# Loads of two chunks moved ahead of a weight load, and other places for a key transpose and for POOL's multiplications, in an RWKV attention with a cosine feed-forward

## The chip, the cores and the metric

The kernel runs on one core of one Trainium2 chip. The metric is the device time of one execution in microseconds, the median of several runs. A core has five engines that work side by side, each through its own queue in order: TensorE (PE, the matmuls), VectorE (DVE), ScalarE (ACT), GpSimd (POOL) and SyncE (SP), which issues the loads and stores here. Loads from one queue are spread over 16 DMA engines, called the rings below.

## The reference

Two parts follow each other. The first is a linear attention with decay over 4 batches, 8 heads, 768 steps and 48 numbers per head; the second takes its output, 3072 tokens of 384 numbers, through two matrices with g = h * cos(h) between them.

```python
for t in range(S):
    kt, vt, rt, wt = (k[:, :, t], v[:, :, t], r[:, :, t], w[:, :, t])
    cur = np.einsum('bhd,bhe->bhde', u[None] * kt, vt)
    y[:, :, t] = np.einsum('bhd,bhde->bhe', rt, state + cur)
    state = wt[:, :, :, None] * state + np.einsum('bhd,bhe->bhde', kt, vt)
...
h = x @ w_in            # 3072 x 384 times 384 x 2048
return (h * np.cos(h)) @ w_out
```

All is float32.

## The kernel before

The steps are cut into 24 chunks of 128 (6 per batch, taken batch by batch within each chunk number, so chunks 0 to 3 are the first of their batches and have no state before them). Two chunks make a block of 256 tokens, and there are 12 blocks.

Attention per chunk j: a load `tt` (L248) holds r, k and w transposed; `v` (L266) holds v; `rk` (L262) holds r and k in natural order for the bonus term with u; `u_sb` (L260) is u, loaded once with the first rk. VectorE makes running products of w from both ends with two scans (e and f in the tables), multiplies r and k by them (r, k), TensorE makes the scores (a, L374 or L382), and VectorE puts them over the diagonal (P). The diagonal comes from r * k (m, L320), times u (u, L321), summed per head on VectorE (c, L325), and spread over a matrix by two selects on POOL (A, L335). For chunks from 4 on, m and u are the only two instructions for the bonus, on POOL in the early part and on VectorE later. The keys are also needed with time on the rows: for chunks from 4 on this is done with 16 small DMAs per chunk (t, L425) and one transpose of 32 x 32 blocks on VectorE (K, L429, output `kn`). The state of a block is made by 64 matmuls from kn and v (s, L444, output `pst`), 32 for each of the two chunks; the block's attention output by o (L479, L485) and p (L507, L513).

Feed-forward per block: 8 units of 256 hidden numbers. A unit is 18 matmuls `ph` (mm1, L594), a chain of five steps I, S, N, M (ScalarE, VectorE, ScalarE, VectorE: rounding to a period, reduction, sine, product), H and L (the result `gs` as a high part, from ScalarE or VectorE, and a low part of two instructions, from POOL, L174), and 12 matmuls `acc` (mm2, L612), of which the first 8 take the high and the last 4 the low part. M frees the PSUM bank that the unit after the next writes. Each float32 operand is split into a high and a low part, therefore three passes per product.

Weights: 16 pieces `raw` of 768 KB (L180), brought into place by two instructions on ScalarE (wg, L195, and wl, L191), a combination on VectorE (wy, L203), a high part (wc, L171) and a low part (wx, L205). Only five pieces of raw memory exist, so that a raw load waits until the piece before it at its place has been converted: weight 14 takes weight 9's place.

The order is written out by hand. For the first two blocks it is the string `START`, whose tokens issue the steps in turn on PE, DVE, ACT and POOL, and the loads on SP. `ld4` is chunk 4's tt load, `v4` its v load, `lr5` chunk 5's rk load with u in front of it if it is the first, `raw14` a weight load; `m5 u5 c5 A5` are the bonus steps of chunk 5. After that, one row per unit of `FIRST` (blocks of the second pass) and then `PLAN`, where `K+3` means K of the chunk 3 behind the block's first. Behind START a scheduler chooses the place of the loads on SP's queue, among them the loads of v and tt for chunks 8 and 9, which `lv+4 lv+5 load+4 load+5` in the first row of FIRST ask for. Buffers are handed out in turn (5 for tt, 4 for v), and a load waits for the last reader of what was there.

The step that prepares a mask for the later chunks hangs on one token:

```python
if n == "u" and j == ALL_OF - 1:
    nc.gpsimd.tensor_copy(out=turned_mask, in_=mask)
```

Of the kernel before, what the change touches and what calls it, by code (L numbers as in the profile page):

```python
# [46 lines left out]
ALL_OF = 6  # L47
# [19 lines left out]
ld0 e0 f0 ld1 raw2 raw1 q0 e1 k0 D14 pc0 r0 q1 cd0 v0 v1 raw0 f1 D10 a0 W0 wg2 wl2 A0 k1 pc1 wl1 r1 wy2 P0 cd1 D6 a1  # L67
wc2 t0 wg1 A1 ld3 ld2 wg0 W1 t1 P1 v5 wx2 wy1 o0 K0 K1 xh0.0 xp0.0 s0 wl0 e3 q3 wc1 xa0.0 wy0 wc0 xh0.1 wp1 f3 pc3
xp0.1 wv1 wx0 xa0.1 q2 e2 n0 k3 f2 raw3 k2 m0.0 m1.0 pc2 t3 r3 I0 r2 wg3 raw4 v2 wl3 cd2 v3 raw5 wy3 m0.1 cd3 S0 t2 a3
A3 K3 K2 A2 P3 ld7 wl4 wg4 a2 ld5 wc3 wg5 N0 raw8 raw6 P2 s1 wx3 raw9 n1 o1 xh1.0 xl1.0 raw7 m1.1 xh1.1 xl1.1 M0 m0.2  # L70
wl5 Wa3 I1 wy4 m1.2 S1 m0.3 H0 wc4 N1 wy5 wc5 wg6 I2 m1.3 M1 wx4 wl6 I3 Hv1 L0 mm2.0 m0.4 wx5 S2 N2 wy6 S3 wg9 wl9 M2
m1.4 N3 L1 mm2.1 H2 I4 e5 wc6 wy9 L2 m0.5 M3 m1.5 S4 H3 wx6 N4 wg7 raw14 v4 L3 ld4 lr5 M4 raw11 m0.6 mm2.2 wl7 wcv9
wy7 wx9 mm2.3 wg8 I5 S5 wc7 wx7 H4 N5 M5 k5 m1.6 m0.7 raw10 W2 wl8 wg11 I6 m1.7 H5 wy8 L4 mm2.4 S6 wc8 L5 I7 N6 S7 N7
wl11 wx8 M6 mm2.5 H6 M7 H7 m0.8 m1.8 m5 u5 wl10 L6 I8 wg10 c5 f5 wy11 m0.9 L7 S8 e4 ld6 raw13 raw12 lr4 m1.9 N8 M8 I9
wc11 wy10 wg12 wc10 mm2.6 mm2.7 raw15 t5 d4 S9 N9 H8 A5 r5 wx11 a5 wx10 M9 wl12 wl13 H9 L8 L9 m0.10 wy12 wc12 m1.10
wg13 m0.11 I10 k4 P5 wx12 S10 m1.11 N10 mm2.8 I11 wy13 M10 wg15 wl15 Wa5 wc13 W4 m4 u4 d5 S11 c4 f4 wx13 N11 M11 m0.12
r4 H10 A4 L10 wg14 mm2.9 m1.12 m0.13 Hv11 K5 t4 wl14 I12 S12 N12 pp4 pp5 m1.13 a4 P4 wy15 L11 I13 M12 wy14 wcv15 S13
wx15 mm2.10 wc14 o2 mm2.11 N13 wx14 p2 m0.14 H12 m1.14 M13 m0.15 L12 xh2.0 Hv13 e6 k6 t6 m1.15 I14 S14 K4 N14 M14
mm2.12 I15 S15 xl2.0 L13 Hv14 L14 mm2.13 xh2.1 N15 s2 xl2.1 M15 Hv15 L15 n2
# [9 lines left out]
LAST = "mm1 I S N M", "mm1 I S N M mm2 h l", "mm2 h l"  # L89
# [7 lines left out]
def rwkv_cos_ffn(ctx: ExitStack, tc: tile.TileContext, tr, tn, tv, u, ut, wts, w, rkw, vst, us, xs, out):  # L97
# [78 lines left out]
    def fetch_weights(f):  # L176

        place = NF + 1 - RING + (f - 1) % RING
        raw[f] = wt.tile([128, 4 * DM], I32, tag=f"w{place}", name="raw")
        E["qf"].dma_start(out=raw[f].bitcast(I16)[:, :8 * DM - 1], in_=wts[f, :, 1:])  # L180
# [55 lines left out]
    def chunk(j):  # L236

        if j not in atts:
            atts[j] = {"j": j, "g": order[j], "b": order[j] // NCB, "c": order[j] % NCB}
        return atts[j]  # L240

    def att_load(j):
        a = chunk(j)
        g = a["g"]
        a["tt"] = tt = buf("tt", [C, TRW], F32)
        half = 1024 + NP // 2 * 129
        for cols in (*(((half, TRW), (1024, half)) if not atts_loaded else ((1024, TRW),)), (512, 1024), (0, 512)) if j < IN_PARTS else ((0, TRW),):
            E["qt"].dma_start(out=tt[:, slice(*cols)], in_=tr[g, :, slice(*cols)])  # L248
        a["tt"] = tt = tt[:R]
        a["r3"] = tt[:, 0:512].rearrange("p (a t) -> p a t", a=NP)  # L250
        a["k3"] = tt[:, 512:1024].rearrange("p (a t) -> p a t", a=NP)
        a["halves"] = not atts_loaded
        atts_loaded.append(j)
        if j == 0:
            E["qt"].dma_start(out=u_by_head, in_=ut)
# [382 lines left out]
    for i in PAIR:  # L638
# [7 lines left out]
                 a=att_scores, t=att_transpose, s=att_state, o=att_own, p=att_past, x=att_x)  # L646
# [64 lines left out]
    def at_first(token):  # L711

        by = re.match(r"(W|H|wc)([av])(\d+)$", token)
        if by:
            name = dict(W="whole", H="gh", wc="whi0")[by[1]]
            usual, E[name] = E[name], dict(a=nc.scalar, v=nc.vector)[by[2]]
            parts.pop((by[1], int(by[3])))()
            E[name] = usual
            return
        if token[:2] == "wp":  # L720
            parts.pop(("wx", int(token[2:])))
        if token[:2] == "wx":
            for x in "wp", "wv":
                parts.pop((x, int(token[2:])))
        if token[:2] == "xp":
            parts.pop(("xl", (int(token[2]), int(token[4]))))
        if token[:2] == "xl":
            for x in "xp", "xa":
                parts.pop((x, (int(token[2]), int(token[4]))))
        n, at, side = re.match(r"(mm2\.|m[01]\.|[a-zA-Z]+)(\d+)(?:\.(\d))?$", token).groups()  # L730
        j = int(at)
        if n == "ld":
            att_load(j)
            att_decay(atts[j])
            seen.update({(j, "load"), (j, "decay"), (j, "x")})
        elif n == "D":
            tags = BANKS[stage[0]]["h"]
            filled = ps.tile([C, C], F32, tag=tags[(turn["h"] + 1) % len(tags)], name="filled")
            for again in range(j):
                nc.tensor.matmul(out=filled, lhsT=ident, rhs=ident, start=True, stop=True)  # L740
        elif n == "raw":
            fetch_weights(j)
            load_weights(j)
        elif n in ("v", "lr"):
            steps[{"v": "lv", "lr": "lr"}[n]](chunk(j))
            seen.add((j, {"v": "lv", "lr": "lr"}[n]))
            if n == "lr":
                att_diag(chunk(j))
                seen.add((j, "diag"))
        elif n == "pc":  # L750
            att_diag(atts[j])
            seen.add((j, "diag"))
        elif n in ("a", "t"):
            steps[n](atts[j])
            seen.add((j, n))
        elif n in ("o", "p", "s"):
            steps[n](j)
            seen.add((j, n))
            if n == "o" and atts[j * BLK]["c"] == 0:
                att_past(j)  # L760
                seen.add((j, "p"))
        elif n in ("m0.", "m1."):
            mm1(j, int(n[1]))
        elif n == "mm2.":
            mm2(j)
        else:
            if n == "d":
                att_dstate(atts[j])
                seen.add((j, "d"))
            parts.pop((n, (j, int(side)) if side else j))()  # L770
            if n == "u" and j == ALL_OF - 1:
                nc.gpsimd.tensor_copy(out=turned_mask, in_=mask)
                nc.gpsimd.memset(turned_mask[:ROW, TURNED:, ROW:], 0)
                nc.gpsimd.memset(turned_mask[ROW:, TURNED:, :ROW], 1)
# [23 lines left out]
    with tc.manual_schedule(engines={ET.PE, ET.DVE, ET.Activation, ET.Pool}):  # L798
# [6 lines left out]
        for t in range(up2, slots + LAG):  # L805
            n = t - up2
# [187 lines left out]
```

## Time and profile before

| what | value |
|---|---|
| median of 3 runs | 506.35 us (505.32 to 506.54) |
| profiled execution, its span | 506.66 us, 505.0 us |
| PE busy | 490.1 us, 97% of the span, 5560 instructions |
| DVE busy | 391.8 us, 78% |
| ACT busy | 257.9 us, 51% |
| POOL busy | 214.3 us, 42% |
| granted PE clock, mean | 0.997 |
| the chain that ended last | PE 82%, DVE 6%, POOL 5%, ACT 4% |

The times of an instruction come from the profiled execution alone. A busy share is a mean over the whole span: the first 100 us, in which weights are converted and two blocks run interleaved, look different from the ten blocks after them, which repeat every 39 us. In the page's row of granted clock all 40 slices show 9 (that is 90% or more of the full speed) but one, which shows 8: the slice from 139 to 151 us.

### The profile page before, as it was taken

Reading aid. Unit: us, or ns where it says so; the run is one execution under the profiler, and the core shown is the slowest. Engines: PE = TensorE matmul, PEld = TensorE weight load, DVE = VectorE, ACT = ScalarE, POOL = GpSimd, SP = SyncE. Lnnn points to the kernel's source line nnn. Section 1 sums busy time; section 2 is a strip of 40 time slices with the busy share of each in tenths; the row PEclk is TensorE's granted clock in tenths of the full one; section 3 lists DMA queues with packets and bytes.
Section 4 is the critical chain, followed back from the end, with each engine's and each line's share of the span. In section 5 each row is a group of like instructions: output and inputs, shape, how many; then the busy total and the mean of one; then the engine's idle time right before and its main releaser. Section 6 shows DMA issues by size and latency. Waiting matters only on the chain.

```text
span 505.0 us, 13533 instructions
## 1 busy us (share of the span) xinstructions
PE 490.1 (97%) x5560; PEld 474.6 (94%) x5560; DVE 391.8 (78%) x684; ACT 257.9 (51%) x443; POOL 214.3 (42%) x278
## 2 busy tenths in 40 slices
PE   8999898999899999999999999999999999999996
PEld 8889897899899999999999999999999999999996
DVE  8999699987959868967967967966967966587632
ACT  3899687435435445445345445435534444544542
POOL 5136399425435244433533524524523633432330
PEclk9999999999989999999999999999999999999999
DMA  8993933423443250351342332233214203023001
GB/s 281 414 394 140 374 100 95 125 57 107 131 143 106 48 193 18 78 160 53 78 143 70 79 102 110 78 85 127 75 42 155 64 4 124 31 65 126 33 1 35
DMA packets 46289, 58.59 MB, mean 116 GB/s; under 512 B 30736, under 2 KB 37392, under 8 KB 46224
## 3 DMA queue, kind: packets, MB, share of 16 engines
q1 hardware_dynamic: 46080, 57.59, 34.6%
q8 instruction: 45, 0.74, 0.6%
q14 instruction: 20, 0.16, 0.1%
q10 hardware_dynamic: 144, 0.10, 0.1%
HBM read 49.80 MB, written 4.72 MB: 108 GB/s over the span
## 4 chain that ended last, share of the span: by engine, by line
PE 82%; DVE 6%; POOL 5%; ACT 4%; issue 3%; DVEq 0%; ACTq 0%; POOLq 0%
PE ph L594 35%; PE acc L612 34%; POOL gs L174 3%; PE pa L382 2%; PE py L479 2%; PE filled L740 2%; PE py L485 2%; PE py L513 1%; PE pst L444 1%; DVE rr L560 1%; PE pa L374 1%; PE py L507 1%; POOL asb L335 1%; DVE tt L289 1%; ACT gs L171 1%
## 5 line engine op out<-in xcount | busy, mean ns | idle before, releaser
L174 POOL TENSOR_TENSOR gs<-rr,gs 128x256 fp32r<-128x256 f32 x188 | 159.0, 867 | 228.1 <-ACT gs L171 221.5
L594 PE MATMUL ph<-xT,w 128*128 128x256 f32 x1728 | 221.6, 282 | 4.2 <-DVE rr L574 2.9
L594 PEld LDWEIGHTS ph<-xT,w 128*128 128x128 f32 x1728 | 213.8, 189 | 8.5 <-issue 4.1
L612 PE MATMUL acc<-w,gs 128*128 128x384 f32 x1152 | 215.4, 337 | 0.7 <-ACT gs L171 0.7
L612 PEld LDWEIGHTS acc<-w,gs 128*128 128x128 f32 x1152 | 196.3, 188 | 1.3 <-ACT gs L171 1.0
L573 ACT ACTIVATE rr<-rr,quarter 128x512 f32<-128x512 f32 x96 | 69.5, 724 | 87.8 <-DVE rr L560 87.8
L560 DVE SCALAR_TENSOR_TENSOR rr<-rr,ph 128x512 f32<-128x512 int32 x96 | 65.5, 682 | 55.4 <-ACT rr L557 54.8
L171 ACT CAST gs<-rr 128x512 fp32r<-128x512 f32 x91 | 56.5, 621 | 71.1 <-DVE rr L574 51.2
L574 DVE TENSOR_TENSOR rr<-rr,ph 128x512 f32<-128x512 f32 x96 | 65.0, 678 | 21.2 <-ACT rr L573 19.3
L557 ACT ACTIVATE rr<-ph 128x512 int32<-128x512 f32 x96 | 57.2, 596 | 46.5 <-PE ph L594 46.1
L335 POOL TENSOR_SCALAR_AFFINE_SELECT asb<-cd 128x512 f32<-128x512 f32 x48 | 38.3, 823 | 47.7 <-DVE cd L325 28.5
L396 DVE COPY_PREDICATED asb<-turned_mask,pa 64x128 f32<-64x128 uint8 (+1 forms) x108 | 33.6, 346 | 2.1 <-POOL asb L335 0.3
L283 DVE TENSOR_TENSOR_SCAN ee<-tt,one_e 112x516 f32<-112x516 f32 (+1 forms) x25 | 32.4, 1298 | 1.2 <-DMA tt<-tr 1.0
L289 DVE TENSOR_TENSOR_SCAN tt<-tt,inj 112x516 f32<-112x516 f32 x24 | 30.3, 1262 | 0.8
L174 DVE TENSOR_TENSOR xT<-py,xT 128x384 fp32r<-128x384 f32 x22 | 11.5, 552 | 18.4 <-ACT xT L171 18.3
L195 ACT ACTIVATE top<-raw 128x768 f16<-128x768 bf16 x16 | 17.4, 1085 | 6.8 <-DMA raw<-wts 6.1
L479 PE MATMUL py<-asb,v 128*32 128x128 f32 x384 | 18.0, 276 | 0.3 <-DVE asb L393 0.2
L171 ACT CAST xT<-py 128x384 fp32r<-128x384 f32 x24 | 10.7, 481 | 14.5 <-PE py L513 10.2
L485 PE MATMUL py<-asb,v 128*32 128x128 f32 x384 | 17.3, 273 | 0.0
L203 DVE CUSTOM_DVE_ANT_0 h<-h,top 128x1536 uint16<-128x1536 uint16 x16 | 15.6, 973 | 0.7 <-ACT h L191 0.6
L171 ACT COPY past<-dd 48x192 f32<-48x192 f32 x40 | 14.0, 349 | 2.7 <-DVE dd L358 2.4
L382 PEld LDWEIGHTS pa<-tt 48*64 48x64 f32 x576 | 12.9, 133 | 2.2 <-issue 2.2
(93 smaller groups left out, 355.7 us busy)
## 6 DMA issues: line engine op xcount, KB each, us to landing
tt<-tr SPq DMA_DIRECT2D x22, 770.5 KB, 6.5
raw<-wts SPq DMA_DIRECT2D x16, 767.8 KB, 8.3
rk<-tn SPq DMA_DIRECT2D x20, 384.0 KB, 4.4
v<-tv SPq DMA_DIRECT2D x24, 224.0 KB, 3.8
ww<-w SPq DMA_DIRECT2D x6, 768.0 KB, 5.1
out<-ob SPq DMA_DIRECT2D x23, 192.0 KB, 2.0
top<-tt SPq DMA_DIRECT2D x112, 16.0 KB, 1.8
top<-tt SPq DMA_DIRECT2D x112, 8.0 KB, 1.8
```

What stands on the lines that cost most here:

```text
L171: (nc.scalar.copy if E[name] is nc.scalar else E[name].tensor_copy)(out=out, in_=in_)
L174: E[name].tensor_tensor(out=out, in0=full, in1=high.bitcast(F32), op=ALU.subtract)
L283: nc.vector.tensor_tensor_scan(out=ee[:, pairs].rearrange("p a t -> p (a t)")[:, ::-1], data0=wp[:, cols][:, ::-1], data1=one_e[:, pairs]. ...
L289: nc.vector.tensor_tensor_scan(out=wp[:, 0:W129], data0=wp[:, 0:W129], data1=inj.rearrange("p a t -> p (a t)"), initial=0.0, op0=ALU.mult, ...
L335: nc.gpsimd.affine_select(out=asb, in_=col.unsqueeze(2).to_broadcast([C, NP, C]), pattern=[[0, 4], [1, C]], compare_op=ALU.is_equal, fill= ...
L396: nc.vector.copy_predicated(*(which(x) for x in (a["asb", h], turned_mask, pa[h])))
L557: nc.scalar.activation(made["rr"].bitcast(I32), ph, AF.Copy, scale=INV2PI / W_SCALE, bias=0.25)
L560: nc.vector.scalar_tensor_tensor(out=made["rr"], in0=made["rr"].bitcast(I32), scalar=-2.0 * math.pi * W_SCALE, in1=ph, op0=ALU.mult, op1=A ...
L573: N=lambda: nc.scalar.activation(made["rr"], made["rr"], AF.Sin, scale=1.0 / W_SCALE, bias=quarter),
L574: M=lambda: nc.vector.tensor_tensor(out=made["rr"], in0=made["rr"], in1=ph, op=ALU.mult), H=high, L=low)
L594: nc.tensor.matmul(out=ph[:, fi], lhsT=wgt[u * FU + fi][:, 0, a, kt * 128:(kt + 1) * 128], rhs=xT[:, b, kt], start=n == 0, stop=n == 3 * K ...
L612: nc.tensor.matmul(out=accs[i][j][:, :DM], lhsT=gs[:, a, fi, j * C:(j + 1) * C], rhs=wgt[u * FU + fi][:, 1, b], start=u == 0 and fi == 0 a ...
```

## The change

Four edits in the tables and one in the code:

- `v4 ld4 lr5` stand behind `raw7`, the fourth of five raw loads in a row, instead of behind `raw14` and `L3`.
- `m5 u5` stand behind `W2` instead of behind `m1.8`; `c5` behind `I7` instead of behind `wg10`; `A5` at the old place of `m5 u5`.
- `m4 u4` stand at the old place of A5, instead of behind `W4`.
- `K+3` moves in FIRST from the end of the sixth row to the end of the fifth, in front of `k+4`.
- The mask is prepared behind `A5` instead of behind `u5`.

```diff
-A3 K3 K2 A2 P3 ld7 wl4 wg4 a2 ld5 wc3 wg5 N0 raw8 raw6 P2 s1 wx3 raw9 n1 o1 xh1.0 xl1.0 raw7 m1.1 xh1.1 xl1.1 M0 m0.2
+A3 K3 K2 A2 P3 ld7 wl4 wg4 a2 ld5 wc3 wg5 N0 raw8 raw6 P2 s1 wx3 raw9 n1 o1 xh1.0 xl1.0 raw7 v4 ld4 lr5 m1.1 xh1.1
...
-         "a+2 a+3 mm1 P+2 P+3 I S e+4 N M mm2 H L k+4",
-         "mm1 I S f+4 N M mm2 H L r+4 load+6 K+3 t+4",
+         "a+2 a+3 mm1 P+2 P+3 I S e+4 N M mm2 H L K+3 k+4",
+         "mm1 I S f+4 N M mm2 H L r+4 load+6 t+4",
...
-            if n == "u" and j == ALL_OF - 1:
+            if n == "A" and j == ALL_OF - 1:
```

SP's queue from the third of the early tt loads on (raw is a weight, tt, v, u_sb and rk are the loads named above):

```order
 L180 DMA raw<-wts 128x3071
 L248 DMA tt<-tr 128x1541 x2
-L180 DMA raw<-wts 128x3071 x5
+L180 DMA raw<-wts 128x3071 x4
 L266 DMA v<-tv 128x448
 L248 DMA tt<-tr 128x1541
 L260 DMA u_sb<-u 128x384
 L262 DMA rk<-tn 128x768
-L180 DMA raw<-wts 128x3071 x2
+L266 DMA v<-tv 128x448 x2
+L180 DMA raw<-wts 128x3071 x3
 L248 DMA tt<-tr 128x1541
```

Weight 14, the last of the five, has moved behind the four loads, and two v loads (of chunks 8 and 9) have come in front of it; further on, a tt load (chunk 8) has moved from behind the first 16 small DMAs to in front of weight 15.

POOL's queue in START (gs are the low parts L, two instructions per unit: units 4 and 5, then 6 and 7; rk the bonus of chunk 5, then of chunk 4; asb the selects A5; turned_mask the mask):

```order
-L174 TENSOR_TENSOR gs<-rr,gs 128x256 x4
 L320 TENSOR_TENSOR rk<-rk 128x384
 L321 TENSOR_TENSOR rk<-rk,u_sb 128x384
+L174 TENSOR_TENSOR gs<-rr,gs 128x256 x4
+L335 AFFINE_SELECT asb<-cd 128x512 x2
 L772 COPY turned_mask<-mask 128x512
 L773 MEMSET turned_mask 64x2x64
 L774 MEMSET turned_mask 64x2x64
 L174 TENSOR_TENSOR gs<-rr,gs 128x256 x4
-L335 AFFINE_SELECT asb<-cd 128x512 x2
+L320 TENSOR_TENSOR rk<-rk 128x384
+L321 TENSOR_TENSOR rk<-rk,u_sb 128x384
```

Chunk 5's multiplications stand in front of the gs of units 4 and 5, its selects in front of those of 6 and 7, and chunk 4's multiplications where the selects were.

VectorE's queue in the fifth and sixth rows of FIRST, before (the row at L429 is K7; L300 and L302 with ee are k8, those without are r8; L288 and L289 are f8; L574 is M and L560 S of the units):

```order
163 L574 TENSOR_TENSOR rr<-rr,ph 128x512
164 L300 TENSOR_TENSOR tt<-tt,ee 112x256
165 L302 TENSOR_TENSOR tt<-tt,ee 112x256
166 L560 SCALAR_TENSOR_TENSOR rr<-rr,ph 128x512
167 L288 RECIPROCAL inj<-ee 112x4
168 L289 SCALAR_TENSOR_TENSOR tt<-tt,inj 112x516
169 L574 TENSOR_TENSOR rr<-rr,ph 128x512
170 L300 TENSOR_TENSOR tt<-tt 112x256
171 L302 TENSOR_TENSOR tt<-tt 112x256
172 L429 STREAM_TRANSPOSE kn<-top_100 128x512
```

And the same place in the change:

```order
164 L574 TENSOR_TENSOR rr<-rr,ph 128x512
165 L429 STREAM_TRANSPOSE kn<-top_100 128x512
166 L300 TENSOR_TENSOR tt<-tt,ee 112x256
167 L302 TENSOR_TENSOR tt<-tt,ee 112x256
168 L560 SCALAR_TENSOR_TENSOR rr<-rr,ph 128x512
```

K7 has moved up by eight instructions, to right behind the first M. On VectorE there is one more move: c5 stands between the two S of units 6 and 7, before wx8 and the two M, instead of behind these.

## Rows read from the trace of the kernel before

**Rows 1.** TensorE's timeline, 57 to 87: start, length, instruction, [idle before, releaser].

```profile
57.00 2.26 PE L612 MATMUL acc<-w,gs 128*128 128x384 f32 x12
59.94 2.35 PE L612 MATMUL acc<-w,gs 128*128 128x384 f32 x12 [0.69 <-ACT gs L171]
63.94 4.44 PE L594 MATMUL ph<-xT,w 128*128 128x256 f32 x36 [1.64 <-DVE rr L574]
...
81.39 1.30 PE L594 MATMUL ph<-xT,w 128*128 128x256 f32 x9 [1.25 <-DVE rr L574]
...
86.03 3.03 PE L594 MATMUL ph<-xT,w 128*128 128x256 f32 x21 [0.55 <-DVE w L205]
```

**Rows 2.** ScalarE's timeline: the wait for a weight load.

```profile
57.87 1.08 ACT L195 ACTIVATE top<-raw 128x768 f16<-128x768 bf16 x1 [3.80 <-DMA raw<-wts]
```

**Rows 3.** SP's timeline: two groups of raw loads, issue and time until the last.

```profile
28.13 16.99 SPq L180 DMA_DIRECT2D raw<-wts  x5
...
47.12 0.97 SPq L180 DMA_DIRECT2D raw<-wts  x2
```

**Rows 4.** Windows: busy per engine (PE, PEld, DVE, ACT, POOL), clock, DMA share, GB/s.

```profile
38.00:40.00 2.00, 2.00 (x19) 2.00 (x18) 1.94 (x3) 1.94 (x4) 1.37 (x1) 1.00 0.07 28
...
46.00:48.00 2.00, 2.00 (x17) 2.00 (x17) 2.00 (x4) 2.00 (x4) 1.85 (x3) 1.00 0.80 298
```

**Rows 5.** TensorE's timeline: the last output matmuls of block 1.

```profile
33.81 0.45 PE L485 MATMUL py<-asb,v 128*32 128x128 f32 x8
```

**Rows 6.** The page's DMA issues: KB each, median us to landing.

```profile
top<-tt SPq DMA_DIRECT2D x112, 16.0 KB, 1.8
```

**Rows 7.** VectorE's timeline: M of units 6 and 7, and chunk 4's sum.

```profile
63.12 1.27 DVE L574 TENSOR_TENSOR rr<-rr,ph 128x512 f32<-128x512 f32 x2
...
82.78 0.55 DVE L325 TENSOR_REDUCE cd<-rk 128x8 f32<-128x384 f32 x1 [0.32 <-POOL rk L321]
```

**Rows 8.** POOL's timeline, 52 to 75.

```profile
52.72 1.89 POOL L174 TENSOR_TENSOR gs<-rr,gs 128x256 fp32r<-128x256 f32 x2 [2.55 <-ACT gs L171]
...
61.36 1.02 POOL L320 TENSOR_TENSOR rk<-rk 128x384 f32<-128x384 f32 x1
62.45 1.59 POOL L321 TENSOR_TENSOR rk<-rk,u_sb 128x384 f32<-128x384 f32 x1
...
65.17 6.49 POOL L174 TENSOR_TENSOR gs<-rr,gs 128x256 fp32r<-128x256 f32 x4
71.63 3.45 POOL L335 TENSOR_SCALAR_AFFINE_SELECT asb<-cd 128x512 f32<-128x512 f32 x2
```

**Rows 9.** TensorE's timeline: state matmuls, units behind them, and units of a later block.

```profile
139.08 0.53 PE L444 MATMUL pst<-v,kn 128*32 128x48 f32 x32 [2.23 <-DVE kn L429]
...
140.14 3.90 PE L594 MATMUL ph<-xT,w 128*128 128x256 f32 x18
143.84 2.31 PE L612 MATMUL acc<-w,gs 128*128 128x384 f32 x12
...
220.58 2.40 PE L594 MATMUL ph<-xT,w 128*128 128x256 f32 x18
222.82 2.25 PE L612 MATMUL acc<-w,gs 128*128 128x384 f32 x12
224.90 2.26 PE L594 MATMUL ph<-xT,w 128*128 128x256 f32 x18
```

**Rows 10.** VectorE's timeline, 133 to 139.

```profile
133.17 0.66 DVE L574 TENSOR_TENSOR rr<-rr,ph 128x512 f32<-128x512 f32 x1
...
135.09 0.69 DVE L560 SCALAR_TENSOR_TENSOR rr<-rr,ph 128x512 f32<-128x512 int32 x1 [0.59 <-ACT rr L557]
...
138.33 0.70 DVE L429 STREAM_TRANSPOSE kn<-top 128x512 f32<-128x512 f32 x1
```

**Rows 11.** Windows, columns as in rows 4.

```profile
141.00:144.00 3.00, 3.00 (x16) 3.00 (x15) 2.11 (x6) 0.11 (x1) 0.00 (x0) 0.51 0.14 20
```

**Rows 12.** SP's timeline: the last twelve small DMAs for K7.

```profile
116.32 8.57 SPq L425 DMA_DIRECT2D top<-tt  x12
```

More of the change, by code (lines that the diff above doesn't have):

```diff
@@ L69 @@
 xp0.1 wv1 wx0 xa0.1 q2 e2 n0 k3 f2 raw3 k2 m0.0 m1.0 pc2 t3 r3 I0 r2 wg3 raw4 v2 wl3 cd2 v3 raw5 wy3 m0.1 cd3 S0 t2 a3
-A3 K3 K2 A2 P3 ld7 wl4 wg4 a2 ld5 wc3 wg5 N0 raw8 raw6 P2 s1 wx3 raw9 n1 o1 xh1.0 xl1.0 raw7 m1.1 xh1.1 xl1.1 M0 m0.2
[L71 to L76, printed above, removed]
+A3 K3 K2 A2 P3 ld7 wl4 wg4 a2 ld5 wc3 wg5 N0 raw8 raw6 P2 s1 wx3 raw9 n1 o1 xh1.0 xl1.0 raw7 v4 ld4 lr5 m1.1 xh1.1
+xl1.1 M0 m0.2 wl5 Wa3 I1 wy4 m1.2 S1 m0.3 H0 wc4 N1 wy5 wc5 wg6 I2 m1.3 M1 wx4 wl6 I3 Hv1 L0 mm2.0 m0.4 wx5 S2 N2 wy6
+S3 wg9 wl9 M2 m1.4 N3 L1 mm2.1 H2 I4 e5 wc6 wy9 L2 m0.5 M3 m1.5 S4 H3 wx6 N4 wg7 raw14 L3 M4 raw11 m0.6 mm2.2 wl7 wcv9
+wy7 wx9 mm2.3 wg8 I5 S5 wc7 wx7 H4 N5 M5 k5 m1.6 m0.7 raw10 W2 m5 u5 wl8 wg11 I6 m1.7 H5 wy8 L4 mm2.4 S6 wc8 L5 I7 c5
+N6 S7 N7 wl11 wx8 M6 mm2.5 H6 M7 H7 m0.8 m1.8 A5 wl10 L6 I8 wg10 f5 wy11 m0.9 L7 S8 e4 ld6 raw13 raw12 lr4 m1.9 N8 M8
+I9 wc11 wy10 wg12 wc10 mm2.6 mm2.7 raw15 t5 d4 S9 N9 H8 m4 u4 r5 wx11 a5 wx10 M9 wl12 wl13 H9 L8 L9 m0.10 wy12 wc12
+m1.10 wg13 m0.11 I10 k4 P5 wx12 S10 m1.11 N10 mm2.8 I11 wy13 M10 wg15 wl15 Wa5 wc13 W4 d5 S11 c4 f4 wx13 N11 M11 m0.12
 r4 H10 A4 L10 wg14 mm2.9 m1.12 m0.13 Hv11 K5 t4 wl14 I12 S12 N12 pp4 pp5 m1.13 a4 P4 wy15 L11 I13 M12 wy14 wcv15 S13
```

## The prediction

> **What bounds the kernel now.** The page first: TensorE is busy 97% of the span, with the clock granted in full except in one stretch, so what can be won is time in which the engine stands still, or runs at the lower clock; no matmul is removed here. The next view is TensorE's timeline with the idle time in front of each piece. Behind 40 us five waits matter: in front of the pieces that start at 59.94, 63.94, 81.39 and 86.03, and in front of the second half of the state matmuls at 139.08, the longest with 2.23 us [rows 1, 9]. From there to the end it stands still twice more, for less than 0.5 us each. Whatever is won at the five places is carried to the end, because TensorE waits for no other engine behind them.
>
> The first two waits (at 59.94 for a gs from ScalarE, at 63.94 for the multiplication M on VectorE) have one cause further back, which ScalarE's timeline shows: it stands still for 3.80 us until 57.87, for a weight load [rows 2]. This is the first conversion of weight 11. SP's timeline shows that load issued behind 47.12 [rows 3], so it took over 10 us to land: it went out right behind v, tt, u and rk (224 + 770 + 192 + 384 KB), and these had themselves waited behind the fifth of the raw loads, weight 14, which goes out only when ScalarE has converted weight 9. SP stood in that run of five from 28.13 to 45.12 [rows 3], with nothing on the DMA rings: 0.07 busy from 38 to 40, while 46 to 48 shows 0.80 [rows 4].
>
> The fifth wait is one of order on VectorE. Key transpose K7 is the last instruction of its stretch there, at 138.33, behind two multiplications, a scan and four half-size multiplications; the state matmuls want it at 136.85, which is 139.08 less 2.23 [rows 9, 10]. [...]
>
> **The change part by part.**
>
> *The loads.* v4, tt4, u and rk5 go out behind the fourth raw load, before 34 us by their place, instead of behind 45.2. The order shows more than the diff says: two v loads of chunks 8 and 9 come along, ahead of weight 14, and tt of chunk 8 comes ahead of weight 15. Six loads now stand in front of weight 14, and SP goes through them in order; the last reader of a buffer that they wait for is block 1's output matmuls, done at 34.26 [rows 5]. So weight 14 still goes out at 45 and weight 11 right behind it, near 45.2. The moved bytes, 1.57 MB and 0.45 MB of v, find empty rings: at the 298 GB/s of 46 to 48 [rows 4] they take 6.8 us, from 38 to 44.8. Weights 14 and 11 take 2.6 us each at that rate, and 1.8 us is what even a small transfer needs from issue to landing [rows 6]: 45.2 + 5.2 + 1.8 = 52.2. ScalarE wants weight 11 at 54.07. The 3.80 us go.
>
> What is late next? ScalarE and VectorE follow at most 3.80 us earlier, so M, which frees the bank for the piece at 63.94, goes from 63.12 [rows 7] to 59.3, and ends at about 60. TensorE without a wait would want that bank at 57.00 + 2 x 2.08 = 61.16 (2.08 is what 12 acc matmuls take, 222.82 to 224.90). A margin of 1.2 us, so both waits go: 63.94 - 61.16 = 2.78 us. Bounds: 0, if weight 11 still lands where it did, and 2.78.
>
> *The waits at 81.39 and 86.03 (1.25 and 0.55).* Here VectorE is late by itself: from M at 63.12 on it works without a pause but for one wait of 0.32, and it takes its start there from a unit of TensorE, so it moves together with TensorE, and the waits stay. Two things can shorten them: the sum at 82.78 waits 0.32 for a multiplication of POOL [rows 7], which now comes earlier, and POOL's selects for chunk 5 leave VectorE's tightest stretch. I take 0.3 for each, 0.6. Bounds: 1.80, if both waits vanish, and -0.9, if the new order puts one more piece of POOL's work (0.87, the page's mean for a gs) in VectorE's way.
>
> *POOL.* Chunk 5's multiplications (1.02 + 1.59) come in front of the gs at 52.72, into the 2.55 us in which POOL stood still until ScalarE had done its part [rows 8]. Cost 0 to 0.1. The selects A5 (3.45) come in front of the four gs at 65.17, which take 6.49. The new chain, from rows: gs of unit 5 done 3.80 earlier than before, at 57.6; A5 to 61.0; the mask (64.04 to 65.17, 1.13) to 62.2; the four gs to 68.7. TensorE wants the third and fourth of them 1.39 (8 of 12 matmuls) into the later unit's acc piece: 61.16, plus 4.3 for the 36 ph matmuls, 2.08 for the acc piece between and 1.39 is 68.9. Just in time, as before (done at 65.17 + 6.49 = 71.66, wanted at 63.94 + 7.77 = 71.7). Cost 0, upper bound 1.0. [...]
>
> *K7.* One transpose of 0.70 us moves to right behind M at 133.17 and ends at about 134.5 [rows 10]. Its last DMAs are issued by 124.89 [rows 12] and land in some 2 us, so they leave it 7 us. It is wanted at 136.85: the wait goes, 2.23 us. On VectorE it stands in front of S at 135.09, which had waited 0.59 for ScalarE: S comes 0.1 later, and the bank that depends on it is wanted only 4 us after that. Cost 0. With the wait, I think, the lower clock goes: 3.70 - 2.24 = 1.46. The five later blocks have the same small matmuls without the wait, and 2.24 us behind them (one is in [rows 9]). Bounds: 0 and 1.46. [...]
>
> **Sum.** 2.78 + 0.6 + 2.23 + 1.46 = 7.07. The profiled execution took 506.66 us, 1.66 of it around its span: 506.66 - 7.07 = 499.59. The median of the runs, 506.35, lies 0.31 below that execution, so the forecast is 499.3.
>
> **The rivals.**
> - All five waits go: 1.80 instead of 0.6, which gives 498.1; with a little more from VectorE, 497.5. For it: some VectorE instructions between 74 and 79 are stretched while POOL works. Against it: POOL's gs work there still. 0.15.
> - The clock still falls near 136: 499.3 + 1.46 = 500.8. For it: the small matmuls in front of that unit load TensorE less than the large ones. Against it: the later blocks. 0.10.
> - The early part fails by half or more, because weight 11 lands behind 55 or POOL's selects make a new wait: 3.69 and at most 1.4 us more are won, 501.3 to 502.7. For it: 2 MB of other loads go out in front. Against it: the empty rings. 0.09.
> - Slower: POOL's multiplications of chunk 5 now stand in front of the gs of unit 4. If rk5 or u landed late, POOL would wait with that gs behind it, and TensorE for the gs. It is wanted at 57.00 + 1.39 = 58.4; less its 1.89 and the 2.61 of the multiplications, the point is 53.9. Every microsecond beyond costs one: at 61 the gain is gone, and from 62.5 on it is slower by over 1.5 us, 507.9. Against it: rk5 goes out before 34, has 6.8 us of bytes before and with it, and would have to take 28 us. 0.03.
> - Nothing changes, 506: ScalarE's wait stays for another load, and K7 finds its DMAs late. Both would have to be so. 0.02.
>
> The forecast has the remaining 0.61, with a range of its own from 498.4 to 500.3.
>
> **Chances.** A measurement of this kernel can tell some 0.3%, 1.5 us, from no change. Faster by more than that: the forecast and the first three rivals, 0.95; within it 0.02; slower 0.03. The range, 497.4 to 501.8, takes in the first two rivals and the better part of the third, and leaves out the loss of a whole part.
>
> **What would show it.** In the changed profile: rings busy from 38 to 44; no wait of ScalarE for a raw load near 54; TensorE without a pause from 50 to 77; POOL with two multiplications before the gs at 52.7; one wait of about 1 us near 78.6; K7 right behind M; no wait inside the state matmuls near 133, and the clock at 1.00 behind them. Wrong would be: weight 11 landing behind 54.5; TensorE waiting for POOL's gs near 68; a clock of 0.5 near 136; VectorE waiting for K7's DMAs.

## The result and the profile after

The changed kernel takes 500.40 us, the median of six runs (499.83 to 500.98), and the kernel before 506.44 us in its six (505.32 to 506.77). The ratio is 0.9884, with an interval from 0.9871 to 0.9897: 1.16% faster. The forecast was 499.3 us with a range from 497.4 to 501.8. The profiled execution after the change took 500.02 us, with a span of 497.9 us against 505.0.

From the page of the kernel after: busy time per engine, the granted clock in 40 slices, and GB/s.

```profile
PE 487.9 (98%) x5560; PEld 472.4 (95%) x5560; DVE 391.8 (79%) x684; ACT 257.4 (52%) x443; POOL 215.6 (43%) x278
...
PEclk9999999999999999999999999999999999999999
...
GB/s 282 414 404 297 325 107 14 133 65 103 105 142 145 19 197 78 18 199 51 43 202 35 56 184 31 79 129 86 73 82 119 65 25 104 33 65 127 34 1 36
```

TensorE has the same 5560 instructions; its 490.1 busy us became 487.9, and the slice with an 8 is gone from the clock. The fourth slice of the transfers (37 to 50 us) carries 297 GB/s, where it was 140 before.

TensorE's waits in the kernel after, added up over the span by what was waited for: us in total, times, longest (the second of the two in the last line stands at the start).

```profile
PE ph L594 <- DVE rr L574: 1.0, 1, 1.0
...
PE pa L374 <- DVE tt L298: 0.6, 2, 0.4
```

Behind the start one wait of 1.0 is left of the five, and one of 0.4 is new. Short stops stand in no such list; they show in how long a piece takes. TensorE's timeline of the kernel after, at the places of [rows 1, 9]:

```profile
53.39 3.90 PE L594 MATMUL ph<-xT,w 128*128 128x256 f32 x27
57.12 4.33 PE L612 MATMUL acc<-w,gs 128*128 128x384 f32 x24
61.29 4.36 PE L594 MATMUL ph<-xT,w 128*128 128x256 f32 x36
...
70.20 1.16 PE L374 MATMUL pa<-tt 48*128 48x128 f32 x16 [0.39 <-DVE tt L298]
...
78.86 1.29 PE L594 MATMUL ph<-xT,w 128*128 128x256 f32 x9 [0.96 <-DVE rr L574]
...
133.04 0.86 PE L444 MATMUL pst<-v,kn 128*32 128x48 f32 x64
...
134.43 2.37 PE L594 MATMUL ph<-xT,w 128*128 128x256 f32 x18
136.64 2.25 PE L612 MATMUL acc<-w,gs 128*128 128x384 f32 x12
```

From 53.39 on the pieces join: the waits at 59.94 and 63.94 are gone. The wait at 81.39 (1.25) is 0.96 at 78.86. The one at 86.03 (0.55) is no longer listed but not wholly gone: the 27 ph matmuls from 82.09 to 85.70 take 3.61 us, where 27 without a stop take 3.15 (53.85 to 57.00 in the kernel before). The 64 state matmuls run in one piece, and the unit behind them takes 2.21 us (134.43 to 136.64) instead of 3.70.

SP's timeline of the kernel after, the stretch of [rows 3]:

```profile
27.94 3.54 SPq L180 DMA_DIRECT2D raw<-wts  x4
31.57 0.39 SPq L266 DMA_DIRECT2D v<-tv  x1
...
33.03 0.40 SPq L262 DMA_DIRECT2D rk<-tn  x1
33.52 1.91 SPq L266 DMA_DIRECT2D v<-tv  x2
44.59 1.28 SPq L180 DMA_DIRECT2D raw<-wts  x3
```

The six loads go out by 35.4 and weight 14 still at 44.6, with weight 11 right behind it. Weight 11 landed 5.9 us after its issue at 45.0. ScalarE's timeline of the kernel after shows no wait in front of the conversion of weight 11, where [rows 2] has 3.80:

```profile
54.56 1.06 ACT L195 ACTIVATE top<-raw 128x768 f16<-128x768 bf16 x1
```

Windows of the kernel after (columns as in [rows 4]): the rings that stood idle from 38 to 40 now carry 410 GB/s there.

```profile
38.00:40.00 2.00, 2.00 (x19) 2.00 (x18) 1.94 (x3) 1.94 (x4) 1.19 (x1) 1.00 1.02 410
```

POOL's timeline of the kernel after, against [rows 8], and then VectorE's in the same stretch:

```profile
49.95 1.73 POOL L320 TENSOR_TENSOR rk<-rk 128x384 f32<-128x384 f32 x1
51.76 1.62 POOL L321 TENSOR_TENSOR rk<-rk,u_sb 128x384 f32<-128x384 f32 x1
53.34 4.93 POOL L174 TENSOR_TENSOR gs<-rr,gs 128x256 fp32r<-128x256 f32 x4
```

```profile
50.73 1.77 DVE L205 TENSOR_TENSOR w<-h,w 128x768 fp32r<-128x768 f32 x1
...
53.02 1.17 DVE L205 TENSOR_TENSOR w<-h,w 128x768 fp32r<-128x768 f32 x1
54.12 0.68 DVE L574 TENSOR_TENSOR rr<-rr,ph 128x512 f32<-128x512 f32 x1
...
67.53 1.18 DVE L358 TENSOR_TENSOR dd<-all_states,ee 112x192 f32<-112x192 f32 x1
```

Chunk 5's multiplications fit in front of the gs, but not for nothing: the first took 1.73 us instead of 1.02, and the two low weight parts on VectorE (L205) beside them took 1.77 and 1.17. The same two instructions in the kernel before took 0.94 each, in VectorE's timeline there:

```profile
50.91 0.94 DVE L205 TENSOR_TENSOR w<-h,w 128x768 fp32r<-128x768 f32 x1
...
52.37 0.94 DVE L205 TENSOR_TENSOR w<-h,w 128x768 fp32r<-128x768 f32 x1
```

The M behind them (L574) ends late, at 54.80, and the ph piece at 53.39 is stretched to 3.73 us (the acc piece follows at 57.12): in the trace one of its weight loads waits 0.20 for the second low part, and another 0.25, until just after the end of that M, which frees the bank.

How far each place on TensorE moved between the two profiles, after minus before, and what the stretch in between gave:

| place (start before, after) | offset | gained in the stretch |
|---|---|---|
| ph piece (53.85, 53.39) | -0.46 | 0.46, a difference from before this place that no edit was meant to make |
| acc piece (57.00, 57.12) | +0.12 | -0.58, VectorE late beside POOL |
| ph piece (63.94, 61.29) | -2.65 | 2.77, the two waits behind the weight load |
| a of a later chunk (72.48, 70.20) | -2.28 | -0.37, the new wait of 0.39 |
| ph piece (81.39, 78.86) | -2.53 | 0.25 |
| ph piece behind 86.03 (88.99, 85.70) | -3.29 | 0.76 |
| state matmuls (136.32, 133.04) | -3.28 | 0 |
| unit behind them, its end (143.84, 136.64) | -7.20 | 3.92, of it 2.23 the wait, 1.49 the unit (3.70 to 2.21), 0.2 the matmuls between |
| end of the span (505.0, 497.9) | -7.1 | -0.1 |

### The profile page after: what moved, and what is told of

Same layout as the page of the kernel before. It is cut to its first block, busy times and chain, and to the rows that moved or that the text cites. A ratio compares the mean times of both kernels' runs of the same rounds, so it can differ in the third digit from the quotient of the medians.

```text
span 497.9 us, 13533 instructions
## 1 busy us (share of the span) xinstructions
PE 487.9 (98%) x5560; PEld 472.4 (95%) x5560; DVE 391.8 (79%) x684; ACT 257.4 (52%) x443; POOL 215.6 (43%) x278
## 4 chain that ended last, share of the span: by engine, by line
PE 91%; DVE 6%; issue 1%; DMA 1%; ACT 1%; SPq 0%; DVEq 0%
PE ph L594 40%; PE acc L612 39%; PE pa L382 3%; PE py L479 2%; PE py L485 2%; PE py L513 1%; PE pst L444 1%; DVE h L203 1%; PE py L507 1%; DVE tt L298 1%; DVE asb L393 1%; DMA tt<-tr 1%; DVE ee L283 1%; DVE w L205 1%; DVE rr L560 1%
## 5 line engine op out<-in xcount | busy, mean ns | idle before, releaser
L560 DVE SCALAR_TENSOR_TENSOR rr<-rr,ph 128x512 f32<-128x512 int32 x96 | 65.6, 683 | 50.2 <-ACT rr L557 47.7
L574 DVE TENSOR_TENSOR rr<-rr,ph 128x512 f32<-128x512 f32 x96 | 65.0, 678 | 21.2 <-ACT rr L573 19.3
L289 DVE TENSOR_TENSOR_SCAN tt<-tt,inj 112x516 f32<-112x516 f32 x24 | 30.1, 1252 | 0.8
L205 DVE TENSOR_TENSOR w<-h,w 128x768 fp32r<-128x768 f32 x15 | 15.3, 1032 | 0.0
```

The lines of the kernel that those rows point to most:

```text
L289: nc.vector.tensor_tensor_scan(out=wp[:, 0:W129], data0=wp[:, 0:W129], data1=inj.rearrange("p a t -> p (a t)"), initial=0.0, op0=ALU.mult, ...
L560: nc.vector.scalar_tensor_tensor(out=made["rr"], in0=made["rr"].bitcast(I32), scalar=-2.0 * math.pi * W_SCALE, in1=ph, op0=ALU.mult, op1=A ...
L574: M=lambda: nc.vector.tensor_tensor(out=made["rr"], in0=made["rr"], in1=ph, op=ALU.mult), H=high, L=low)
```

## The experiments

Each ran beside the kernel before; ratios are against that.

### The parts apart

**e1: the loads alone.**

```diff
-... xh1.0 xl1.0 raw7 m1.1 ...  wg7 raw14 v4 L3 ld4 lr5 M4 raw11 ...
+... xh1.0 xl1.0 raw7 v4 ld4 lr5 m1.1 ...  wg7 raw14 L3 M4 raw11 ...
```

> Only the loads are moved (v4, tt4, u, rk5 behind the fourth raw load); POOL's order and K7 stay as before. Theory A (the late weight 11 alone made TensorE's waits at 59.94 and 63.94): ScalarE's wait of 3.80 us at 57.87 is gone, both waits of TensorE are gone (2.8 us), the waits near 81 and 86 (1.25 and 0.55) and that for K7 (2.23, with the lower clock behind it) stay: 506.4 - 2.8 = 503.6. Rival B (moving the loads isn't enough, since chunk 5's multiplications still run on POOL at their old place, behind the gs of unit 5): TensorE still waits near 61 to 66, and 1 us or less is won: 505.5.

502.95 us (502.19 to 504.35), ratio 0.9944 (0.9917 to 0.9971). ScalarE's wait is gone, and TensorE's timeline of this kernel has no wait in front of the 36 ph matmuls. At K7 the old wait and the long unit are still there:

```profile
61.55 4.36 PE L594 MATMUL ph<-xT,w 128*128 128x256 f32 x36
...
136.45 0.54 PE L444 MATMUL pst<-v,kn 128*32 128x48 f32 x32 [2.24 <-DVE kn L429]
...
137.51 3.92 PE L594 MATMUL ph<-xT,w 128*128 128x256 f32 x18
```

**e2: K7 alone.**

```diff
-         "a+2 a+3 mm1 P+2 P+3 I S e+4 N M mm2 H L k+4",
-         "mm1 I S f+4 N M mm2 H L r+4 load+6 K+3 t+4",
+         "a+2 a+3 mm1 P+2 P+3 I S e+4 N M mm2 H L K+3 k+4",
+         "mm1 I S f+4 N M mm2 H L r+4 load+6 t+4",
```

> Only K7 is moved, in front of k8. Theory A (the wait for K7 and the lower clock behind it, 2.23 + 1.46): the wait inside the state matmuls is gone, the clock stays at 1.00 behind them, 506.4 - 3.7 = 502.7. Rival B (the small matmuls before that unit lower the clock, not the wait): the wait goes but the clock is near 0.5 for some 3 us, 504.2.

503.10 us (501.88 to 503.36), ratio 0.9942 (0.9920 to 0.9964). The early waits stay (0.89, 1.64, 1.26 and 0.55 in its profile); the state matmuls run in one piece, and the unit behind them takes 2.37 at the full clock.

**e3: both, with POOL's queue as before.** The diffs of e1 and e2 together.

> Loads and K7 moved, POOL's multiplications, selects and mask as before. Theory A (POOL's new places win what the forecast said, 0.6 us): 0.6 slower than the changed kernel, 501.0. Theory B (read from the profile after: POOL's new places cost TensorE 0.58 us near 55 and 0.39 at 70.2 by slowing VectorE, and win 1.0 near 79 to 83): within 0.3 of the changed kernel, without a stretched ph piece at 53 and without a wait at 70, but with waits of 1.25 and 0.55 at about 78.7 and 83.3.

499.79 us (499.55 to 500.31), ratio 0.9885 (0.9859 to 0.9912): as fast as the whole change. TensorE's timeline of this kernel shows that the two differ all the same:

```profile
53.94 3.31 PE L594 MATMUL ph<-xT,w 128*128 128x256 f32 x27
...
70.00 1.16 PE L374 MATMUL pa<-tt 48*128 48x128 f32 x16 [0.21 <-DVE tt L298]
...
79.02 1.29 PE L594 MATMUL ph<-xT,w 128*128 128x256 f32 x9 [1.34 <-DVE rr L574]
```

Without POOL's moves the ph piece near 54 isn't stretched (3.31 for 27 matmuls) and the wait at 70 is 0.21 instead of 0.39, but the wait near 79 is 1.34 instead of 0.96. What POOL's new places win at 79 and 82 (0.56 us by the places) they lose at 55 and 70 (0.58 and 0.18).

**e4: POOL's and c5's new places alone**, the loads and K7 as before. It makes the condition of the slower rival true: rk5 lands late, with a gs behind the multiplications that wait for it.

```diff
-... raw10 W2 wl8 ... L5 I7 N6 ... m1.8 m5 u5 wl10 L6 I8 wg10 c5 f5 ... H8 A5 r5 ... wc13 W4 m4 u4 d5 ...
+... raw10 W2 m5 u5 wl8 ... L5 I7 c5 N6 ... m1.8 A5 wl10 L6 I8 wg10 f5 ... H8 m4 u4 r5 ... wc13 W4 d5 ...
-            if n == "u" and j == ALL_OF - 1:
+            if n == "A" and j == ALL_OF - 1:
```

> POOL's new order (and c5's place on VectorE) with the loads where they were before, K7 as before: the slower rival of the prediction made true. Theory A: rk5 lands at about 56.1, POOL waits for it with the gs of unit 4 behind it until 56.1 + 2.6 + 1.9 = 60.6 while TensorE wants that gs at 58.4; TensorE waits 2.2 us for POOL there, in place of part of the old waits: between 506.5 and 508.7. Rival B (the weight load behind it stays the bound, and POOL's wait hides in ScalarE's): within 0.5 of before.

505.73 us in ten runs (504.04 to 506.52), ratio 0.9984 (0.9968 to 1.0001): no clear difference. Its spans are shorter all the same, 503.65 us in the median against 504.7 in the 15 of the kernel before that ran beside it; 0.4 us of its time is a longer stretch around the span, which comes up below. POOL's timeline of this kernel has the wait that the rival spoke of, and TensorE's has what came of it:

```profile
55.09 1.61 POOL L320 TENSOR_TENSOR rk<-rk 128x384 f32<-128x384 f32 x1 [4.56 <-DMA rk<-tn]
```

```profile
60.21 2.36 PE L612 MATMUL acc<-w,gs 128*128 128x384 f32 x12 [0.34 <-ACT gs L171]
...
63.81 4.44 PE L594 MATMUL ph<-xT,w 128*128 128x256 f32 x36 [1.24 <-DVE rr L574]
```

POOL stands still for 4.56 us until 55.09, 1.2 us past the point of 53.9 that I had worked out, yet TensorE waits less than in [rows 1]. The same late transfers hold ScalarE for 3.71 us in this kernel, so TensorE's work is late by itself and POOL's wait lies beside that. For the slower rival to cost its price rk5 would have to be late and weight 11 in time; no run has both with POOL's new places, so that price is not shown.

### Why the loads' move works

**e9: the order turned round.** Weights 14, 11 and 10 first and the four loads behind them, all as late as in the kernel before; the rings stay as idle from 38 to 44 as they were.

```diff
-... wg7 raw14 v4 L3 ld4 lr5 M4 raw11 m0.6 ...  m0.7 raw10 W2 ...
+... wg7 raw14 raw11 raw10 v4 ld4 lr5 L3 M4 m0.6 ...  m0.7 W2 ...
```

> The kernel before, with weights 11 and 10 issued right behind weight 14 and ahead of v4, tt4, u, rk5; nothing uses the empty stretch of the rings from 38 to 45. Theory A (what delayed ScalarE is weight 11's place behind 1.57 MB in the queue, not the empty rings as such): weight 11 lands near 51 to 52, ScalarE's wait of 3.7 us goes as it did when the loads moved, and the time is that of the kernel with only the loads moved, 503 to 503.6; rk5 and tt4 land near 60, and if POOL's multiplication or VectorE's scan has to wait for them, a us is lost again near 64. Rival B (the rings have to be emptied early, since all transfers share them): ScalarE still waits over 2 us, 505.5.

503.82 us in ten runs (502.33 to 506.42), ratio 0.9963 (0.9943 to 0.9983); the kernel before had a median of 505.16 beside it, for a reason that the part on the clock gives. ScalarE's wait is gone here too, and TensorE joins up from 54 to 68. So what held weight 11 back was the 1.57 MB queued ahead of it (its conversion starts at 54.58 here without a wait; in the kernel before it landed 10.7 us after its issue at 47.1, and the conversion starts at 57.87); the idle rings only gave these bytes a time at which they cost nothing. The four loads now come late instead, which POOL's timeline of this kernel shows (first), and at K7 the old wait stands, in TensorE's timeline (second) with a full clock behind it:

```profile
59.32 1.28 POOL L320 TENSOR_TENSOR rk<-rk 128x384 f32<-128x384 f32 x1 [1.20 <-DMA rk<-tn]
```

```profile
136.55 0.54 PE L444 MATMUL pst<-v,kn 128*32 128x48 f32 x32 [2.23 <-DVE kn L429]
...
137.61 2.37 PE L594 MATMUL ph<-xT,w 128*128 128x256 f32 x18
```

### The wait and the clock

**e7: the wait filled.** The kernel before, with 17 matmuls of an identity in the place of K7's wait, written to a part of the PSUM bank that nothing reads.

```diff
-        pst = bank("a", [C, BLK, NP, HD], "pst") if two else None
+        held = bank("a", [C, 512], "pst") if two else None
...
+            if i == 3 and n == 1:
+                for again in range(17):
+                    nc.tensor.matmul(out=held[:, 384:], lhsT=ident, rhs=ident, start=True, stop=True)
```

> The kernel before, with 17 matmuls of 128 columns (identity times identity, into 128 free columns of the state's bank, read by nobody) between the two halves of block 3's state matmuls, about the 2.2 us that TensorE stands still there. Theory A (standing still makes the clock fall): the clock stays at 1.00, the next unit takes 2.24 instead of 3.70, 506.4 - 1.5 = 504.9, with K7 still late. Rival B (the small matmuls before it lower the clock, or something else there): the clock falls to 0.5 all the same, 506.4 or a little more.

506.20 us in ten runs (505.82 to 506.62), ratio 0.9999 (0.9986 to 1.0011). The 504.9 of theory A did not come, because I had made the filling too long: it took 4.06 us, 1.8 more than the wait of 2.23. TensorE's timeline of this kernel:

```profile
137.13 4.06 PE L442 MATMUL pst<-ident 128*128 128x128 f32 x34
...
142.18 2.37 PE L598 MATMUL ph<-xT,w 128*128 128x256 f32 x18
144.39 2.25 PE L616 MATMUL acc<-w,gs 128*128 128x384 f32 x12
```

With work in the wait the unit behind takes 2.21 us, and the 1.8 us too much are about paid for by the 1.5 us that the full clock gives back: from the first state matmul to the acc piece it takes 7.72 us, the kernel before 7.52. None of its ten executions has a mean clock under 0.998. (The waits of this kernel near 81 and 86 are 0.73 and 1.46 instead of 1.25 and 0.55; why is open.)

**e5: half a wait.** The kernel after, with `K+3` in the sixth row behind `f+4`, which leaves K7 behind one M, two multiplications of k8, an S and the scan.

```diff
-         "a+2 a+3 mm1 P+2 P+3 I S e+4 N M mm2 H L K+3 k+4",
-         "mm1 I S f+4 N M mm2 H L r+4 load+6 t+4",
+         "a+2 a+3 mm1 P+2 P+3 I S e+4 N M mm2 H L k+4",
+         "mm1 I S f+4 K+3 N M mm2 H L r+4 load+6 t+4",
```

> The changed kernel with K7 behind f8, one scan and two half multiplications later than in the change, so that TensorE waits about 1 us for it instead of 0 or 2.23. Theory A (the clock falls with the length of the standstill): a wait of 0.9 to 1.1 us and a clock of 1.00 behind it, 500.4 + 1.0 = 501.4. Rival B (any standstill among these small matmuls is enough): the wait of 1 us and the slow unit of 3.7 us behind it, 502.9.

500.54 us in four runs (500.15 to 501.72), ratio 0.9907 (0.9874 to 0.9939). TensorE's timeline of this kernel:

```profile
134.29 0.54 PE L444 MATMUL pst<-v,kn 128*32 128x48 f32 x32 [0.95 <-DVE kn L429]
...
135.35 2.37 PE L594 MATMUL ph<-xT,w 128*128 128x256 f32 x18
```

A wait of 0.95 us costs itself and no clock: from the first state matmul to the unit 2.53 us, against 1.39 in the changed kernel. The 501.4 of the expectation did not come. The median of the spans is 498.8, against 498.35 in the change, and the stretch around the span is 0.4 shorter in this kernel.

**before_look1 and before_look2: the kernel before, unchanged, twice more**, because e9 had the full wait and the full clock.

> The kernel before, unchanged, one more profile. So far the clock fell to 0.5 behind the wait of 2.23 us in three profiles of four that have it. Theory A (the same wait lets the clock fall in some executions and not in others): sooner or later a profile of it shows the unit behind the wait at 2.24 instead of 3.70, and its time is then about 1.5 us below the others, near 505. Rival B (it always falls in this kernel, and the one profile without a fall differs in its earlier part): 3.70 and 0.5 again, 506.5.

> As before_look1: by theory A a clock of 1.00 or 0.5 behind the wait, with times 1.5 us apart; by rival B 0.5.

506.74 and 506.77 us. Windows of the first and of the second, clock third from the end:

```profile
139.00:141.00 2.00, 2.00 (x67) 1.55 (x56) 0.20 (x1) 0.71 (x2) 0.66 (x1) 0.60 0.16 24
141.00:144.00 3.00, 3.00 (x20) 3.00 (x19) 2.15 (x6) 0.34 (x2) 0.00 (x0) 0.70 0.12 17
```

```profile
139.00:141.00 2.00, 1.84 (x69) 1.58 (x70) 0.26 (x2) 0.67 (x2) 1.04 (x2) 0.94 0.13 21
141.00:144.00 3.00, 3.00 (x16) 3.00 (x15) 2.19 (x6) 0.20 (x1) 0.00 (x0) 0.50 0.16 22
```

The clock fell in both, at places 1 to 2 us apart, so no profile of the unchanged kernel shows it staying up. Of six profiles with the wait of 2.2 us (before, these two, e1, e4 and e9) five show the fall. How often it comes is told by the timed executions, each of which lists its mean granted clock. Of 44 of the kernel before, 30 have 0.997 or less, as its profiles with the fall have, and a median of 506.57 us; 13 have 0.999 or 1.000, and a median of 504.95 (one lies between). The means do not say where the clock fell, but the difference, 1.62 us, is near the 1.46 of the forecast's term. And they go with the wait: of 69 executions of the kernels that have it (the kernel before, e1, e4, e9) 44 have 0.997 or less, and of 41 of the kernels without it (the change, e2, e3, e5, e6, e8, and e7 with the wait filled) none has, the lowest being 0.998. The share moves the median of the kernel before: 11 of 15 beside e1 to e4 (506.40), 10 of 13 beside e6 to e8 (506.20), but 6 of 13 beside e5 and e9 (505.16), so the gains of these two look smaller.

### Other places for POOL's work

**e6: the kernel after, with chunk 5's multiplications behind the gs of unit 4 instead of in front of it, and chunk 4's back at their old place.**

```diff
-... W2 m5 u5 wl8 ... wy8 L4 mm2.4 ...  H8 m4 u4 r5 ... W4 d5 ...
+... W2 wl8 ... wy8 L4 m5 u5 mm2.4 ...  H8 r5 ... W4 m4 u4 d5 ...
```

> The changed kernel with chunk 5's multiplications on POOL behind the gs of unit 4 instead of in front of it, and chunk 4's back behind W4. Theory A (POOL's multiplications in front of that gs slow VectorE's low part wx from 0.94 to 1.77 and so M, and TensorE loses 0.58 near 55; chunk 4's, where they are, stretch d4 to 1.18 and cost 0.39 at 70.2): both losses go, 0.6 to 1.0 us faster than the changed kernel, 499.4. Rival B (the collisions move along with the instructions): same, and a wait of 0.5 turns up near 83 instead.

500.47 us (500.15 to 500.71), ratio 0.9883 (0.9866 to 0.9899). The stretched piece is gone, as meant, and of the loss near 70 half is left: from the 36 ph matmuls in front of it to the a at 70.34 it takes 8.74 us, against 8.91 in the change and 8.54 in the kernel before. The wait of the kernel before is back behind them. TensorE's timeline of this kernel:

```profile
54.23 3.31 PE L594 MATMUL ph<-xT,w 128*128 128x256 f32 x27
...
79.37 1.30 PE L594 MATMUL ph<-xT,w 128*128 128x256 f32 x9 [1.35 <-DVE rr L574]
```

**e8: e6, with S10 and M10 each in front of a weight step on VectorE.**

```diff
-... k4 P5 wx12 S10 m1.11 N10 mm2.8 I11 wy13 M10 wg15 ...
+... k4 P5 S10 wx12 m1.11 N10 mm2.8 I11 M10 wy13 wg15 ...
```

> As e6_pool_order, and on VectorE S of unit 10 goes in front of wx12, M of unit 10 in front of wy13. Theory A (the wait near 78.9 is VectorE's order: S10 stands 0.9 behind its input, and M10 behind wy13): that wait of 0.96 goes too, 1.6 to 1.9 faster than the changed kernel, 498.6. Rival B (VectorE is short of time as a whole there): the wait comes back in front of the next units, same as e6_pool_order.

500.28 us (500.24 to 500.34), ratio 0.9879 (0.9862 to 0.9895). The wait is shorter, and two new ones stand behind it, for the weight parts that were put off. TensorE's timeline of this kernel:

```profile
78.32 1.29 PE L594 MATMUL ph<-xT,w 128*128 128x256 f32 x9 [0.60 <-DVE rr L574]
...
82.04 0.97 PE L594 MATMUL ph<-xT,w 128*128 128x256 f32 x6 [0.34 <-ACT w L171]
83.28 3.05 PE L594 MATMUL ph<-xT,w 128*128 128x256 f32 x21 [0.27 <-DVE w L205]
```

Nothing is won: the waits listed add up to 1.21, against 1.35 in e6, but from the a near 70 to the next one (70.05 to 86.26) it takes 16.21 us, in e6 16.07 (70.34 to 86.41).

**after_again: the changed kernel once more**, beside e6, e7 and e8.

> The changed kernel once more, beside the next three: all theories say 500.0 to 500.5.

500.51 us (500.25 to 500.62), ratio 0.9882 (0.9865 to 0.9898). Nothing tried here is clearly faster than the change: e3 has the lowest median (499.79), most of it for a reason that comes up below.

## Why the prediction was right, and where it was not

**The loads.** Right, step by step: weight 14 at 44.6 (forecast 45), weight 11 landed near 50.9 (forecast at the latest 52.2), no wait of ScalarE, both waits of TensorE gone, 2.77 us in the table against 2.78. e1 shows that the move alone does it. One reason was off: I named the idle rings beside the queue in front of weight 11. e9 leaves them as idle and ScalarE's wait goes all the same, so the queue was the cause.

**POOL.** "Cost 0 to 0.1" for chunk 5's multiplications is the step that failed: they cost 0.58 near 55 us. In one more profile with the same places, after_again, the ph piece takes 3.40 us (54.17 to 57.57), 0.25 more than without a stop, and in e3 and e6, without them, 3.15; so the loss is not the same in every execution. I had looked for who waits for POOL, and found the 2.55 us in which it stood still. What hid the cost from me was the other direction, VectorE beside POOL: 1.77 and 1.17 instead of 0.94 twice, and an M that frees its bank late. Chunk 4's multiplications, whose cost I had left out of the sum, overlap the instruction at 67.53 (1.18 us; 0.90 before, 0.78 in e3), and the wait of 0.39 at 70.20 stands behind it. Half of the 0.37 lost there is theirs: e3 and e6, without them, lose 0.19 and 0.20. Of the signs that I had named, TensorE without a pause from 50 to 77 did not come.

Beside POOL's work the same instruction of VectorE took different times: L205 0.94 or 1.77 us, L358 0.35 with POOL idle (another of the same size, at 78.63 in the kernel after), 0.90 beside a gs (at 70.16 in the kernel before) and 1.18 beside the multiplications. POOL's own differ too: the four gs at 65.17 took 1.62 each, the two at 52.72 0.95 each [rows 8], with VectorE at work beside both. Not every overlap cost VectorE something: the L205 at 52.37 in the kernel before kept its 0.94 with a gs from 52.72 on. What makes the difference is not shown.

**The waits at 81.39 and 86.03.** 0.25 and 0.76 came, about 1.0, between the 0.6 and the 1.80 of the first rival. The 0.6 was meant for POOL's moves, and that size was about right; what failed is that the waits would otherwise stay. From the a at 72.48 to the next at 88.99 the kernel before takes 16.51 us, e3 16.06, e1 16.09 and the change 15.50: 0.45 came with the loads, without POOL's moves, and 0.56 with them. Why the loads help here is open; e9, whose four loads come late, has 16.55. What POOL's moves brought they had lost before, 0.56 won against 0.58 and 0.18 lost in this profile. By the medians of e3, e6, e8 and the whole change, 499.79 to 500.51, and by those of their spans, 498.05 to 498.4, POOL's order is worth nothing that can be measured; without its 0.6 the sum of the prediction would have ended at 499.9.

**K7 and the clock.** The wait of 2.23 us went, by e2 alone as well, and K7's DMAs were there. The clock's term was right in size: 1.46 forecast, from the 3.70 and 2.24 us for a unit's 18 ph matmuls in [rows 9], with 0.51 of the clock granted from 141 to 144 [rows 11]; about 1.5 in the profile, 1.62 between the two groups of executions. It isn't in every execution of the kernel before: 30 of 44 have the lower mean clock, 0.997 or less, and e9's profile has the same wait of 2.23 us and a granted clock of 1.00 in all its windows from 133 to 142. That the fall goes with this standing still is shown by e7 (filled: no mean clock under 0.998 in ten executions) and e5 (0.95 us: 1.00 from 132 to 138), and by the counts of 44 in 69 and none in 41.

**The sum and the median.** The span fell by 7.1 us, where the sum said 7.07; in that agreement errors cancel: 0.58 + 0.37 lost near 55 and 70, against 0.4 more from the waits near 81 and 86, 0.2 more around K7 and 0.46 from before 53 us, which no edit was meant to make. That is luck. The median fell by 6.0 only, and the forecast is 1.1 too low: 500.40 is inside the whole range, but 0.1 above the forecast's own (498.4 to 500.3). It lies near the 500.8 of the second rival, which is not what happened: the clock stayed up. Three things make up that 1.1. The time around the span is 2.1 us in the profiled execution instead of 1.66, 0.44 more; the median before lay 0.31 below its profiled execution, which I carried over; the median after lies 0.38 above its own (0.44 + 0.31 + 0.38 = 1.13).

The first of the three belongs to the built kernel: all 10 executions of the changed one have 2.05 to 2.22 around the span, those of the kernel before 1.66 to 1.76, e2, e4, e6 and e8 2.04 to 2.21, e3, e5, e7 and e9 1.66 to 1.82, and e1 1.79 to 1.86. Most of the 0.6 by which e3 lies below the whole change is this. What makes it is open; no edit goes with it (e2 and e3 share K7's move, e5 has all of POOL's moves). The rest is spread: ten spans after the change lie between 497.7 and 498.9, with a median of 498.35, and the start alone, to the first ph piece behind the blocks' attention near 34 us, differs by 1.1 between profiles (33.77 in e5, 34.83 in e9). Between the kernel after (34.01) and e9 it is 0.82, and there it stands in SP's raw loads near 28 us already (27.94 and 28.75), before the first load that an edit moved; the kernel before alone has 33.88 to 34.29 in its three profiles. What sets that start is open too.

## What to carry to other kernels

Before a wait for a load is put down to bandwidth, add up what stands in front of it in its own queue, and look for the stretch in which the queue's issuer is itself held: the loads that are free of that hold belong in front of it (here 1.57 MB in front of weight 11, and SP held in one run of loads from 28.13 to 45.12 us). A gap in one engine's timeline is a free place for work only if nothing beside it is stretched (here an L205 of VectorE from 0.94 to 1.77 us); price both sides, and follow the stretched instruction to the engine that bounds the kernel. And where a lower clock was seen behind a wait (here 0.51 behind 2.23 us), add the clock's cost (here about 1.5 us), but read from the executions' own clocks in how many it was there (here 30 of 44): the median moves with that part.

## What the runs showed of the hardware

- The same wait of 2.2 us between small matmuls was followed by a lower clock in five profiles and not in a sixth (e9); a wait of 0.95 us was not followed by one in its profile (e5).
- The fall comes at no fixed distance: the window from 139 to 141 has 0.60 in one profile of the kernel before and 0.94 in another, with the same wait in front.
- 17 matmuls of 128 x 128 x 128 in float32 stand as 34 records and take 4.06 us in e7, 0.24 each, nearly twice what I had reckoned for filling the wait of 2.23.
- Weight 11 took over 10 us to land behind 1.57 MB and the rest of a weight in its own queue, and 5.9 us behind one other weight (the kernels before and after).
- The time around the span differs between builds of nearly the same program by about 0.4 us (near 1.7 or 2.1, in e1 1.8), and by 0.2 at most among the executions of one.
- VectorE's L358 (112 x 192) took 0.35 us with POOL idle and up to 1.18 beside POOL's multiplications (the kernel after); VectorE's L205 kept 0.94 where a gs of POOL started 0.35 us behind it (the kernel before).
